# Moving the table matmuls, the gate parts and the first table's store in an attention and mixture-of-experts kernel

## The chip, the cores and the metric

The kernel runs on one core of a Trainium2 chip. The metric is the device time of one execution in microseconds. A core has TensorE (PE in the profile; PEld is its weight load), VectorE (DVE), ScalarE (ACT), GpSimd (POOL) and SyncE (SP). Each engine works through its own instructions in order. SyncE and GpSimd also issue the transfers (DMA) between DRAM and on-chip memory.

## What is computed

The reference is attention followed by a mixture of experts with one expert per token. Cut to what matters:

```
# attention: 8 batches, 8 heads, 576 positions, 64 wide
scores = q @ k.T / 8, masked (heads 0-3: the last 32 positions; heads 4-7: every 32nd)
x = softmax(scores) @ v                       # 4608 tokens x 512

do_compute = x @ w_skip > 0
logits     = xc @ w_gate                      # 8 experts
e_idx      = argmax(logits);  gate_w = softmax(logits)[e_idx]
for e in range(8):
    h = relu(xc[e_idx == e] @ w1[e])          # 512 -> 1024
    y[e_idx == e] = gate_w * (h @ w2[e])      # 1024 -> 512
out = x;  out[do_compute] = xc + y
```

## The kernel before

**The attention part** is a loop over 32 units: 8 batches (`b`) of 4 units (`pr`), where units 0 and 1 hold the heads with the local mask and units 2 and 3 those with the strided one. An iteration `n` mixes three units: the scores of unit n+2 (`qk`, L201, into the bank S), the transposes and exponentials of unit n (`tex`, L239 and L247), and the product with v of unit n-1 (`pv`, L273). VectorE adds the mask (L208, L210), which empties S, takes the maximum (L216), and divides the product by its sum (L281 to L288). GpSimd subtracts the maximum (L219). TensorE, VectorE and GpSimd are under a manual schedule here, so that their order is the order of the code.

**Routing** lies between these. A group of batches is routed when it is done: groups are batches 0-1, 2-3, 4, 5, 6 and 7 (`GROUPS`). `score` (L331) multiplies with the gate weights, `route1` makes logits, exponentials and the chosen expert on VectorE, `norm` (L386 to L388, GpSimd) adds up the exponentials into `gate`, and `route2` (L394 to L406) ranks the tokens of each expert by matmuls.

**The tables.** For each expert a table on chip (`tabs`) lists its tokens: row to read, row to write, gate weight. It is made by matmuls. `hot` (up to five tiles of 128 tokens) makes on VectorE two one-hots of a token's place, `eh` (L433) and `lo` (L445), from `hq` and `hc` (L428 to L431). It also takes the reciprocal of the gate sum (L435), which GpSimd splits into three bf16 parts (L437 to L440); GpSimd then multiplies `eh` with five columns (place, tile, three gate parts) into `hpm` (L442). `place` (L452) multiplies `lo` with `hpm` on TensorE and VectorE adds the result to `acc` (L456, L458). The list `ready` holds what `hot` has made at the end of an iteration; the next iteration places it. `tabled` (L463 to L468) turns `acc` into `tabs`.

**The tail.** The fullest expert among the first groups, "e", is computed first (`ffn1`, `ffn2`, L648 to L650), from a table of up to 288 tokens read before the last groups are known. When all groups are placed, its whole table is stored to DRAM (L977) and 128 rows behind its first ones are read back from there as a list "l" (`listed`, L613), since the place is known only at run time. `gather` (L620, GpSimd) fetches the tokens' rows, `xsplit` (L642) transposes them, and `tok1` and `tok2` compute the list. The other seven experts follow in the order of `TURN`, each with its table read by `rows` (L610) and its own gathers. Weights come in pieces of 512 KB through three buffers `raw` (`wdma`, L567, SyncE), which VectorE frees by `wrest` (L584). In the tail the scheduler orders SyncE and GpSimd; TensorE, ScalarE and VectorE stand as written.

Of the kernel before, what the change touches and what calls it, by code (L numbers as in the profile page):

```python
# [37 lines left out]
NP = 5  # L38
# [70 lines left out]
def attn_moe(ctx: ExitStack, tc: tile.TileContext, q, k, v, w9d, w1d, w2d, cst, out, NB=B):  # L109
# [279 lines left out]

    def route2(g, tag="T", of=None):  # L390
# [30 lines left out]
    def hot(a, z):  # L421
# [5 lines left out]
        q, c, r = sp("hq", []), sp("hc", []), sp("hr", [])  # L427
# [7 lines left out]
        V.reciprocal(gate[:, o], gate[:, o])  # L435
        w = [parts[:, o, i] for i in range(2, NP)]
        G.tensor_copy(w[0], gate[:, o])  # L437
        G.tensor_tensor(r, gate[:, o], w[0], op=ALU.subtract)
        G.tensor_copy(w[1], r)
        G.tensor_tensor(w[2], r, w[1], op=ALU.subtract)  # L440
# [395 lines left out]
    late, ranked, warm, ready = [], None, [], []  # L836
    pool_order = ExitStack()
    pool_order.enter_context(tc.manual_schedule(engines={G.engine, T.engine, V.engine}))
    for n, (b, pr) in enumerate(units):
# [30 lines left out]
        full = bool(ready) and ready[0][0] == GOFF[GROUPS.index((CB, CB + 1))]  # L870
        put = [] if full and pr == 0 else [place(*x) for x in ready]
        if put:
            ready = []
# [13 lines left out]
        if full and pr == 1:  # L887
            run(*put)
            tabled()
# [29 lines left out]
        if n == 1:  # L919
            G.tensor_copy(parts[:, :, 0:2], con["pk"].rearrange("p (t c) -> p t c", c=2))  # L920
        if warm and pr == (0 if warm[0][0] not in GOFF else 3 if warm[0][0] >= GOFF[GROUPS.index((CB, CB + 1))] else 2):
            ready.append(hot(*warm.pop(0)))
# [21 lines left out]
    psum, bufs = pctx.enter_context(tc.tile_pool(name="psumT", bufs=1, space=PSUM, reuse_waits="tile")), {"S": 2, "T": 3, "PV": 2, "R": 1}  # L944
    ga = ffn1a("e")
# [4 lines left out]
    run(islice(g, 4), *[place(*x) for x in ready], later(route1, nr), islice(g, 4), later(route2, nr))  # L950
    norm(nr)
    new = hot(*hots(nr)[0])
# [18 lines left out]
    s0n = nc.sync.value_load(isel[0:1, 2:3], min_val=0, max_val=(NE - 1) * ESTR + CE[0] * CE[1])  # L971
    for r in TURN:
        e = nc.sync.value_load(order[0:1, 0, r:r + 1], min_val=0, max_val=NE - 1)
        seq += [(r, e, j) for j in range(8)]
        if r == TURN[0]:
            wdma(*seq[2], 1)
            nc.sync.dma_start(tvw[bass.ds(e0, 1), 0:CMAX, :].rearrange("o (p h) c -> p (o h c)", h=3),  # L977
                              tabs[:, bass.ds(e0, 1)].rearrange("p o h c -> p (o h c)"))
        rows(r, e, *CAPS[r])
        if r == TURN[1]:  # L980
            listed("l", s0n)
    done = [0]
# [154 lines left out]
```

## Time and profile before

| | |
|---|---|
| timed runs | 463.47, 464.99, 459.25 us; median 463.47 |
| profiled execution | 461.03 us, of it the span 458.8 us |
| busy share of the span | PE 90%, DVE 61%, ACT 41%, POOL 30% |
| mean granted TensorE clock | 0.966 |
| attention part | 0 to about 190 us, the tail from there to the end |
| moved | 90.39 MB, 197 GB/s |

A row of the timeline gives the start (us from the span's start), the duration, the engine, the line, the operation with its output and inputs, and how many were merged; in brackets the idle time of the engine ahead of it and who ended it. A row of the waits view gives who waited for whom: total, times, longest. "SPq" is a transfer's issue on SyncE. The share of busy time hides that the first 190 us and the tail have different limits.

### The profile page before, as it was taken

What the parts mean: (1) busy time and instruction counts of PE and PEld (TensorE: products, weight loads), DVE (VectorE), ACT (ScalarE), POOL (GpSimd) and SP (SyncE); (2) the same over time, 40 slices, a digit from 0 to 9 for tenths busy, and PEclk for the clock granted to TensorE, in tenths of its full rate; (3) what the DMA queues carried; (4) which work ended last, traced back from release to release, by engine and by line L of the source; (5) the groups of instructions that cost most, each with busy time, mean ns of one, the idle gap of its engine ahead of it and who ended that gap; (6) DMA issues with size and microseconds to landing.
All of it is one profiled execution on the core that took longest, in us unless ns stands there. A gap on an engine that the chain in (4) does not pass through costs nothing.

```text
span 458.8 us, 12154 instructions
## 1 busy us (share of the span) xinstructions
PE 412.3 (90%) x4983; PEld 369.5 (81%) x4984; DVE 279.1 (61%) x584; ACT 187.0 (41%) x366; POOL 138.1 (30%) x190
## 2 busy tenths in 40 slices
PE   6989889889788777997999999999999999999990
PEld 3867767667576565787999799999999999999980
DVE  4666768766998878491477465464574655746410
ACT  1344354416254436541543243443543545444300
POOL 3333224541455455133113416023023030201110
PEclk8899999879999799999999999999999999999996
DMA  8999998978796323513547467556475565644110
GB/s 299 395 389 320 367 328 285 306 226 269 224 351 225 101 53 105 146 46 79 191 155 208 154 212 207 144 185 184 160 228 154 189 192 195 224 139 152 28 39 21
DMA packets 53032, 90.39 MB, mean 197 GB/s; under 512 B 9479, under 2 KB 29191, under 8 KB 52973
## 3 DMA queue, kind: packets, MB, share of 16 engines
q1 hardware_dynamic: 46541, 79.21, 52.3%
q0 software_dynamic: 6432, 10.37, 8.2%
q8 instruction: 40, 0.66, 0.6%
q14 instruction: 19, 0.16, 0.1%
HBM read 75.16 MB, written 14.92 MB: 196 GB/s over the span
## 4 chain that ended last, share of the span: by engine, by line
PE 67%; DVE 13%; DMA 9%; issue 3%; POOL 3%; ACT 2%; SPq 1%; POOLq 0%; DVEq 0%; ACTq 0%
PE S L648 15%; PE S L649 15%; PE S L650 15%; PE PV L273 5%; PE T L239 4%; PE S L201 3%; DMA vt<-in_vp_dram 3%; DVE x L288 2%; PE T L315 2%; PE T L331 2%; PE PV L740 2%; DVE mx L216 2%; PE T L642 1%; DMA kt<-in_kp_dram 1%; DMA xg<-out_dram,tab 1%
## 5 line engine op out<-in xcount | busy, mean ns | idle before, releaser
L648 PE MATMUL S<-xh,w1h 128*128 128x342 f32 (+6 forms) x248 | 78.4, 316 | 0.0
L649 PE MATMUL S<-xl,w1h 128*128 128x342 f32 (+6 forms) x248 | 76.4, 308 | 0.0
L650 PE MATMUL S<-xh,w1l 128*128 128x342 f32 (+6 forms) x248 | 76.4, 308 | 0.0
L728 POOL DMA_INDIRECT out_dram<-ot,tab x25 | 27.9, 1118 | 149.2 <-DVE ot L726 135.5
L648 PE MATMUL S<-hh,w2h 128*128 128x288 f32 (+5 forms) x192 | 59.3, 309 | 0.1
L649 PE MATMUL S<-hl,w2h 128*128 128x288 f32 (+5 forms) x192 | 57.9, 302 | 0.0
L650 PE MATMUL S<-hh,w2l 128*128 128x288 f32 (+5 forms) x192 | 57.8, 301 | 0.0
L660 ACT ACTIVATE hh<-S 128x342 fp32r<-128x342 f32 (+6 forms) x64 | 28.0, 437 | 65.7 <-PE S L650 59.3
L584 DVE TENSOR_TENSOR w1l<-raw,w1h 128x1024 fp32r<-128x1024 f32 x32 | 39.6, 1244 | 21.6 <-ACT w1h L578 21.6
L648 PEld LDWEIGHTS S<-xh,w1h 128*128 128x128 f32 x248 | 46.8, 189 | 0.6 <-issue 0.4
L649 PEld LDWEIGHTS S<-xl,w1h 128*128 128x128 f32 x248 | 46.9, 189 | 0.1
L650 PEld LDWEIGHTS S<-xh,w1l 128*128 128x128 f32 x248 | 46.8, 189 | 0.0
L219 POOL TENSOR_TENSOR sm<-sm,mx 128x480 f32<-128x480 f32 (+1 forms) x32 | 28.4, 907 | 57.2 <-DVE mx L216 28.1
L620 POOL DMA_INDIRECT xg<-out_dram,tab x25 | 31.2, 1248 | 46.5 <-DMA tab<-table 12.6
L584 DVE TENSOR_TENSOR w2l<-raw,w2h 128x1024 fp32r<-128x1024 f32 x32 | 39.0, 1224 | 9.8 <-ACT w2h L578 9.6
L661 DVE SCALAR_TENSOR_TENSOR hl<-S,hh 128x342 fp32r<-128x342 f32 (+6 forms) x64 | 30.9, 484 | 19.9 <-ACT hh L660 19.7
L201 PE MATMUL S<-kt,qt 64*64 64x54 f32 (+1 forms) x1280 | 34.3, 248 | 9.6 <-DMA kt<-in_kp_dram 3.6
L201 PEld LDWEIGHTS S<-kt,qt 64*64 64x64 f32 x1280 | 28.2, 145 | 16.8 <-DVE sm L208 4.2
L648 PEld LDWEIGHTS S<-hh,w2h 128*128 128x128 f32 x192 | 36.2, 188 | 0.4 <-DVE hl L661 0.4
L645 DVE TENSOR_TENSOR xl<-T,xh 128x288 fp32r<-128x288 f32 (+7 forms) x30 | 13.1, 468 | 38.3 <-ACT xh L644 38.3
L649 PEld LDWEIGHTS S<-hl,w2h 128*128 128x128 f32 x192 | 36.2, 189 | 0.0
L650 PEld LDWEIGHTS S<-hh,w2l 128*128 128x128 f32 x192 | 36.2, 189 | 0.0
(178 smaller groups left out, 807.5 us busy)
## 6 DMA issues: line engine op xcount, KB each, us to landing
raw<-in_w_dram SPq DMA_DIRECT2D x64, 512.0 KB
vt<-in_vp_dram SPq DMA_DIRECT2D x40, 390.0 KB
qt<-in_qp_dram SPq DMA_DIRECT2D x16, 304.0 KB
kt<-in_kp_dram SPq DMA_DIRECT2D x16, 297.0 KB
out_dram<-x SPq DMA_DIRECT2D x16, 288.0 KB
kt<-in_kp_dram SPq DMA_DIRECT2D x14, 304.0 KB
qt<-in_qp_dram SPq DMA_DIRECT2D x14, 288.0 KB
out_dram<-x SPq DMA_DIRECT2D x32, 99.0 KB
```

The source lines that it names most:

```text
L201: T.matmul(s[HP * (i ^ j):HP * (i ^ j) + HP, j, (blk - b0) * win:(blk - b0 + 1) * win], lhsT=qt[p, j, blk * nq:blk * nq + HP], rhs=kt[p, j ...
L219: G.tensor_tensor(e[:, j], sw[:, j], mx[:, j].unsqueeze(2).broadcast_to([128, b1 - b0, win]), op=ALU.subtract)
L239: T.transpose(t[:w, x * 128:(x + 1) * 128], a, ident)
L273: T.matmul(p[HP * i:HP * i + HP, bank, slot * 65:slot * 65 + 65], lhsT=pt[a:z, m, j, i ^ j, :], rhs=vt[a:z, (b0 if kind == 0 else b0 // 2) ...
L584: V.tensor_tensor(lo, raw_.pop((key, j)), hi.bitcast(F32), op=ALU.subtract)
L620: i = G.indirect_dma_start(out=xg[:s["P"], t, :], out_offset=None, in_=out[0:last, :], in_offset=bass.IndirectOffsetOnAxis(ap=s["tab"][:s[ ...
L648: T.matmul(p, lhsT=a[0], rhs=b[0], start=start, stop=False)
L649: T.matmul(p, lhsT=a[0], rhs=b[1], start=False, stop=False)
L650: T.matmul(p, lhsT=a[1], rhs=b[0], start=False, stop=stop)
L660: A.activation(s["hh"][:, f, :C], p[:, :C], AF.Relu)
L661: V.scalar_tensor_tensor(s["hl"][:, f, :C], p[:, :C], 0.0, s["hh"][:, f, :C].bitcast(F32), op0=ALU.max, op1=ALU.subtract)
L728: i = G.indirect_dma_start(out=out, in_=ot[:P], in_offset=None, bounds_check=NTOK - 1, oob_is_err=False, out_offset=bass.IndirectOffsetOnA ...
```

## The change

It has four parts.

1. A `place` now waits one iteration longer behind its `hot`, that is two in all, except for group 2 (batch 4), which stays at one.
2. The reciprocal and the three gate parts leave `hot` and become `gates`, done for a whole group at once: for batches up to 5 an iteration after the group's `norm`, for later ones right behind `norm`.
3. The store of the first expert's table and the read of the list "l" are issued by GpSimd instead of SyncE.
4. SyncE reads the seven expert numbers first, and then all tables but the first.

```diff
+    def gates(g):
+        o, nt = slice(GOFF[g], GOFF[g + 1]), tiles(g)
+        zs = gate[:, o]
+        w, r = [parts[:, o, i] for i in range(2, NP)], ap.tile([128, GT], F32, name="rr", tag="rr", bufs=1)[:, 0:nt]
+        V.reciprocal(zs, zs)
+        G.tensor_copy(w[0], zs)
+        G.tensor_tensor(r, zs, w[0], op=ALU.subtract)
+        G.tensor_copy(w[1], r)
+        G.tensor_tensor(w[2], r, w[1], op=ALU.subtract)
...
     def hot(a, z):
...
-        V.reciprocal(gate[:, o], gate[:, o])
-        w = [parts[:, o, i] for i in range(2, NP)]
-        G.tensor_copy(w[0], gate[:, o])
-        G.tensor_tensor(r, gate[:, o], w[0], op=ALU.subtract)
-        G.tensor_copy(w[1], r)
-        G.tensor_tensor(w[2], r, w[1], op=ALU.subtract)
...
-        full = bool(ready) and ready[0][0] == GOFF[GROUPS.index((CB, CB + 1))]
-        put = [] if full and pr == 0 else [place(*x) for x in ready]
-        if put:
-            ready = []
+        put = [x for x in ready if n - x[0] > (x[1] != GOFF[GROUPS.index((CB - 1, CB))])]
+        ready = [x for x in ready if x not in put]
+        full = bool(put) and put[0][1] == GOFF[GROUPS.index((CB, CB + 1))]
+        put = [place(*x[1:]) for x in put]
...
-        if full and pr == 1:
+        if full:
             run(*put)
             tabled()
...
+        if summed_up:
+            gates(summed_up.pop())
+        if g and pr == 3:
+            if b > CB:
+                gates(g[0])
+            else:
+                summed_up.append(g[0])
...
-            ready.append(hot(*warm.pop(0)))
+            ready.append((n, *hot(*warm.pop(0))))
...
+    s0n = G.value_load(isel[0:1, 2:3], min_val=0, max_val=(NE - 1) * ESTR + CE[0] * CE[1])
...
-    run(islice(g, 4), *[place(*x) for x in ready], later(route1, nr), islice(g, 4), later(route2, nr))
+    run(islice(g, 4), *[place(*x[1:]) for x in ready], later(route1, nr))
     norm(nr)
+    gates(nr)
+    run(islice(g, 4), later(route2, nr))
...
-    s0n = nc.sync.value_load(isel[0:1, 2:3], min_val=0, max_val=(NE - 1) * ESTR + CE[0] * CE[1])
+    G.dma_start(tvw[bass.ds(s0, 1), 0:CMAX, :].rearrange("o (p h) c -> p (o h c)", h=3),
+                tabs[:, bass.ds(s0, 1)].rearrange("p o h c -> p (o h c)"))
+    listed("l", s0n, eng=G)
+    eids = {}
     for r in TURN:
-        e = nc.sync.value_load(order[0:1, 0, r:r + 1], min_val=0, max_val=NE - 1)
+        eids[r] = e = nc.sync.value_load(order[0:1, 0, r:r + 1], min_val=0, max_val=NE - 1)
         seq += [(r, e, j) for j in range(8)]
         if r == TURN[0]:
+            rows(r, e, *CAPS[r])
             wdma(*seq[2], 1)
-            nc.sync.dma_start(tvw[bass.ds(e0, 1), 0:CMAX, :].rearrange("o (p h) c -> p (o h c)", h=3),
-                              tabs[:, bass.ds(e0, 1)].rearrange("p o h c -> p (o h c)"))
-        rows(r, e, *CAPS[r])
-        if r == TURN[1]:
-            listed("l", s0n)
+    for r in TURN[1:]:
+        rows(r, eids[r], *CAPS[r])
```

Where the instructions stand is set by these lists, so three places are shown in the engines' order. In the changed kernel the line numbers are a little higher: L452 is L456, L442 is L446, L435 is L394, L388 stays.

TensorE, in batch 3, where the first table matmuls stand; before:

```order
L273 MATMUL PV<-vt_981,pts 64x65 x24
L315 MATMUL T<-cs,x_1327 128x128 x4
L452 LDWEIGHTS hlo
L452 MATMUL T<-hpm,hlo 128x120
...
L201 MATMUL S<-kt_1290,qt_1287 64x54 x24
L239 MATMUL T<-cs,sm_85 96x128 x10
L273 MATMUL PV<-vt_981,pts 64x65 x20
L315 MATMUL T<-cs,x_1512 128x128 x6
L201 MATMUL S<-kt_1290,qt_1287 64x54 x20
```

And in the change:

```order
L273 MATMUL PV<-vt_981,pts 64x65 x24
L315 MATMUL T<-cs,x_1333 128x128 x4
L201 MATMUL S<-kt_1296,qt_1293 64x54 x24
L239 MATMUL T<-cs,sm_85 96x128 x10
L273 MATMUL PV<-vt_981,pts 64x65 x20
L315 MATMUL T<-cs,x_1512 128x128 x6
L456 LDWEIGHTS hlo
L456 MATMUL T<-hpm,hlo 128x120
...
L201 MATMUL S<-kt_1296,qt_1293 64x54 x20
```

The five matmuls stand an iteration later, behind the next scores, transposes and product. The same holds for the three other `hot`s of the first two groups; the matmuls of the later groups keep their places.

VectorE, in batch 6 (unit 3), where the group of batch 5 is ranked; before:

```order
L406 TENSOR_REDUCE rank<-rdd 128x5
L428 TENSOR_SCALAR hq<-rank 128x5
L429 TENSOR_SCALAR hq<-hq 128x5
L430 TENSOR_TENSOR hc<-hq,pickw 128x5
L431 SCALAR_TENSOR_TENSOR hc<-hc,rank 128x5
L433 TENSOR_TENSOR heh<-cs,hc 128x120
L435 RECIPROCAL gate<-gate 128x5
L445 TENSOR_TENSOR hlo<-cs,hq 128x640
L210 TENSOR_TENSOR sms<-S,cs 128x648
```

And in the change:

```order
L416 TENSOR_REDUCE rank<-rdd 128x5
L394 RECIPROCAL gate<-gate 128x5
L438 TENSOR_SCALAR hq<-rank 128x5
L439 TENSOR_SCALAR hq<-hq 128x5
L440 TENSOR_TENSOR hc<-hq,pickw 128x5
L441 SCALAR_TENSOR_TENSOR hc<-hc,rank 128x5
L443 TENSOR_TENSOR heh<-cs,hc 128x120
L449 TENSOR_TENSOR hlo<-cs,hq 128x640
L210 TENSOR_TENSOR sms<-S,cs 128x648
```

The reciprocal has moved from behind the one-hot `heh` to the front of the five instructions that make it.

GpSimd, at the end of the routing; before, the last product `hpm` is followed by the gathers:

```order
L442 TENSOR_TENSOR hpm<-heh,parts 128x600
L620 DMA xg<-out_dram,tab 128x512
L620 DMA xg<-out_dram,tab 114x512 x3
L728 DMA out_dram<-ot,tab 4608x512
L620 DMA xg<-out_dram,tab 114x512 x3
```

And in the change:

```order
L446 TENSOR_TENSOR hpm<-heh,parts 128x600
L985 ISA
L985 DMA table<-tabs 128x12
L617 ISA
L617 DMA tab<-table 128x4
L624 DMA xg<-out_dram,tab 128x512
L624 DMA xg<-out_dram,tab 114x512 x3
```

The store and the read of the list stand between the product and the gathers; SyncE has lost both.

More of the change, by code (lines that the diff above doesn't have):

```diff
@@ L425, in sp @@
             return ap.tile([128, RT1] + shape, dt, name=n, tag=n, bufs=1)[:, 0:nt]
-        q, c, r = sp("hq", []), sp("hc", []), sp("hr", [])
+        q, c = sp("hq", []), sp("hc", [])
         V.tensor_scalar(q, rank_[:, o], -1.0, 1.0 / 3.0, op0=ALU.add, op1=ALU.mult)
@@ L835, in attn_moe @@
     tvw = table.rearrange("(e r) c -> e r c", e=NE)
-    late, ranked, warm, ready = [], None, [], []
+    late, ranked, warm, ready, summed_up = [], None, [], [], []
     pool_order = ExitStack()
```

## The prediction

> **What bounds the kernel now.** I read the busy time by stretches first, one stretch for each batch of the attention part, cut where TensorE starts the score matmuls (L331). The columns are the stretch, its length, busy microseconds (and instructions) of PE, PEld, DVE, ACT and POOL, the granted clock, the DMA share and GB/s.
>
> ```profile
> 39.63:58.31 18.68, 16.86 (x388) 13.32 (x385) 11.92 (x26) 8.17 (x18) 6.20 (x8) 1.00 0.97 336
> 77.86:102.80 24.94, 20.72 (x401) 16.93 (x398) 17.68 (x42) 8.28 (x18) 11.02 (x19) 0.81 0.84 275
> 102.80:123.75 20.95, 18.36 (x410) 14.35 (x410) 16.15 (x46) 9.19 (x22) 6.88 (x12) 0.98 0.75 229
> 123.75:145.46 21.71, 17.90 (x413) 14.25 (x410) 20.52 (x54) 10.09 (x23) 12.79 (x23) 1.00 0.91 321
> 145.46:170.32 24.86, 18.85 (x369) 15.01 (x366) 20.08 (x55) 10.99 (x24) 11.35 (x21) 0.86 0.32 90
> 220.00:300.00 80.00, 79.51 (x493) 73.86 (x492) 43.94 (x68) 33.99 (x57) 20.80 (x16) 1.00 0.62 183
> ```
>
> A batch without table work takes 18.68 us. I call the next four (78 to 170 us) A, B, C and D; the table work of the first two groups lies in A and C. In A nothing is full: TensorE is busy for 20.72 of 24.94 us, and at a clock of 0.81. In C VectorE is busy for 20.52 of 21.71 us, so there it is the bound. Who waits, by the waits view (total, times, longest):
>
> ```profile
> PE T L452 <- POOL hpm L442: 7.2, 4, 2.3
> PE T L452 <- DVE pickw L372: 2.2, 1, 2.2
> PE T L642 <- DMA xg<-out_dram,tab: 2.8, 2, 2.6
> ```
>
> TensorE stands 9.4 us before the table matmuls (L452) and 2.8 us before the transposes of gathered rows (L642), 2.6 of it in one piece at 214.71 us. These are what the change aims at. Past that last wait TensorE is the bound: 79.51 of 80 us in the last row of the stretches.
>
> **Part 1, batch A.** The timeline of its two stalls (start, duration, engine, operation; in brackets the idle time ahead and its releaser):
>
> ```profile
> 83.47 0.95 DVE L208 TENSOR_TENSOR sm<-S,cs 128x768 f32<-128x768 f32 x1
> 85.76 0.42 PE L452 MATMUL T<-hpm,hlo 128*128 128x120 bf16 x5 [1.97 <-POOL hpm L442]
> 86.11 1.11 PE L201 MATMUL S<-kt,qt 64*64 64x54 f32 x48
> 87.15 2.37 PE L239 MATMUL T<-cs,sm 128*96 128x128 f32 x10
> 95.37 0.71 DVE L210 TENSOR_TENSOR sms<-S,cs 128x540 f32<-128x540 f32 x1
> 97.46 0.56 PE L452 MATMUL T<-hpm,hlo 128*128 128x120 bf16 x4 [2.25 <-POOL hpm L442]
> 97.95 1.88 PE L201 MATMUL S<-kt,qt 64*64 64x96 f32 x40
> 132.86 1.30 PE L239 MATMUL T<-cs,sm 128*96 128x128 f32 x10
> 142.79 1.05 PE L201 MATMUL S<-kt,qt 64*64 64x96 f32 x40
> ```
>
> With the matmuls an iteration later, TensorE goes from L315 straight to the next L201. That needs the S bank, which VectorE empties by 84.42 (83.47 + 0.95) and by 96.08 (95.37 + 0.71). L201 so starts 1.7 us earlier instead of at 86.11, and 1.9 us earlier instead of at 97.95: 3.6 us in all. Then the clock: the same ten transposes take 2.37 us behind the first stall and 1.30 in C, the same forty matmuls 1.88 behind the second and 1.05 in C.
>
> ```profile
> 82.00:86.00 4.00, 2.03 (x60) 1.61 (x58) 3.86 (x10) 1.44 (x3) 2.83 (x6) 1.00 1.02 365
> 86.00:90.00 4.00, 4.00 (x82) 3.36 (x81) 1.74 (x3) 1.46 (x3) 1.61 (x2) 0.59 1.08 391
> 98.00:102.00 4.00, 4.00 (x64) 3.45 (x65) 1.44 (x2) 0.00 (x0) 1.24 (x2) 0.50 0.79 254
> ```
>
> Half-busy stretches are followed by 0.59 and 0.50. With idle pieces of about 0.6 and 0.9 us in place of 2.0 and 2.2 I expect the clock to stay up. That gives 1.07 + 0.83 on these two rows, and at a clock of 0.50 half of the other 2.1 us up to 102 us, 1.1: 3.0 in all. The moved copy of the sum costs back 0.3, since it now stands ahead of the next one-hots on VectorE. Raw sum 6.3. It can't all be had: VectorE's 17.68 us stay, and C shows that a batch takes at least 1.2 us more than VectorE's busy time (21.71 - 20.52). So A goes from 24.94 to about 19.0: **-5.9 us**, with bounds -6.3 and -3.3 (the stalls without the clock).
>
> [...]
>
> **Part 2, batches B, C, D.** In B the reciprocal of the gates (0.2 us, as the row of L435 below) stands alone on VectorE's chain, with no work to hide it: **+0.2**. In C:
>
> ```profile
> 140.40 0.71 DVE L210 TENSOR_TENSOR sms<-S,cs 128x540 f32<-128x540 f32 x1
> 142.49 0.37 PE L452 MATMUL T<-hpm,hlo 128*128 128x120 bf16 x4 [1.97 <-POOL hpm L442]
> 149.79 1.39 DVE L584 TENSOR_TENSOR w1l<-raw,w1h 128x1024 fp32r<-128x1024 f32 x1 [1.77 <-ACT w1h L578]
> 151.63 2.82 SPq L296 DMA_DIRECT2D out_dram<-x  x2
> 157.23 1.02 DVE L288 TENSOR_TENSOR x<-PV,rc 128x384 f32<-128x384 f32 x2
> ```
>
> L201 can start at 141.11 instead of 142.79, so TensorE runs 1.7 us ahead. VectorE is full here, and gets only what it waited for: 1.77 us for ScalarE's cast, which stands behind TensorE's score matmuls. SyncE issues the store (L296) once that VectorE instruction has freed a weight buffer, and the product at 157.23 waits for the store. I take **-1.2** (bounds 0 and -1.7), carried along that chain into D. The table matmul of group 2 (the wait of 2.2 us) stays in its iteration; its product hpm starts sooner, and it lies beside the same store, so it adds nothing.
>
> In D the reciprocal moves ahead of the one-hots:
>
> ```profile
> 151.10 0.16 DVE L428 TENSOR_SCALAR hq<-rank 128x5 f32<-128x5 f32 x1
> 151.97 0.28 DVE L433 TENSOR_TENSOR heh<-cs,hc 128x120 bf16<-128x120 f32 x1
> 161.76 0.24 POOL L388 TENSOR_SCALAR gate<-gate 128x5 f32<-128x5 f32 x1
> 162.03 0.19 DVE L435 RECIPROCAL gate<-gate 128x5 f32<-128x5 f32 x1 [0.41 <-POOL gate L388]
> ```
>
> Now VectorE does the five one-hot instructions while GpSimd makes the gate sum, and waits only 0.41 us. In the change it meets the reciprocal first, waits until 162.0, and does the five after it. Queued behind it are hq to heh (151.10 to 152.25, 1.15 us), hlo and the mask of the next scores, for which TensorE waits. I price it at 1.15 less 0.05: **+1.1** (bounds +0.3, if GpSimd comes sooner, and +1.3).
>
> **Part 3, the tail.** First VectorE's chain to the table, then the transfers:
>
> ```profile
> 195.18 0.23 POOL L388 TENSOR_SCALAR gate<-gate 128x5 f32<-128x5 f32 x1
> 199.91 1.17 DVE L482 SCALAR_TENSOR_TENSOR key<-cnt,cs 1x8 f32<-1x8 f32 x1
> 201.11 0.15 DVE L519 SCALAR_TENSOR_TENSOR key<-first,key 1x8 f32<-1x8 f32 x1
> 204.43 0.20 DVE L468 TENSOR_TENSOR tabs<-tat,acc 128x24 f32<-128x24 f32 x1
> 172.28 0.78 POOL L610 DMA_DIRECT2D tab<-tabs  x1 [1.13 <-DVE tabs L468]
> 213.67 1.13 POOL L620 DMA_INDIRECT xg<-out_dram,tab  x1 [12.61 <-DMA tab<-table]
> 217.32 0.44 PE L642 MATMUL T<-cs,xg 128*128 128x128 f32 x2 [2.61 <-DMA xg<-out_dram,tab]
> ```
>
> ```profile
> 206.77 4.51 DMA table<-tabs
> 211.30 1.59 DMA tab<-table
> ```
>
> The key instruction of eight elements (L482) takes 1.17 us while GpSimd makes the product hpm, and the like one behind it (L519) 0.15. In the change the four GpSimd instructions ahead of hpm are done before, so hpm no longer meets it: 1.0 won. The reciprocal now stands ahead of the last ranks and waits for the gate sum, done at 195.41, where VectorE went on at about 195.2: with its own time some 0.4 lost. So tabs is done at 204.0 instead of 204.63. SyncE issued its store at 206.77, behind a weight load; GpSimd has nothing in front of it and I let it start at 204.35 (0.35 later). The store takes 4.5 as now, the load back 2.0 (1.59, and 0.4 since GpSimd's issue took 0.78 in the row of L610), with 0.3 and 0.8 between: the first gather starts at 212.0 instead of 213.67. The gathers of the second expert follow it at a fixed distance and release TensorE last, so all of it counts: **-1.7**. SyncE's seven register loads and table reads are as many as before; they lie beside TensorE's matmuls, and the weight load behind them now goes out sooner.
>
> ```profile
> DMA to landing us min/median/max: 2.7/4.7/8.2
> ```
>
> This row of the tables' transfers bounds a small one from both sides. With 2.7 and 2.0 the gain is 3.5; with 4.7 for both it is a loss of 1.2.
>
> [...]
>
> **Sum:** -5.9 + 0.2 - 1.2 + 1.1 - 1.7 = -7.5 us. The profiled execution took 461.03 us (span 458.8 and 2.2 around it), which gives 453.5. The three other runs are 459.25, 463.47 and 464.99; the mean of the four is 462.2, and I forecast from that: **454.7 us**.
>
> **The rivals.**
>
> The clock does not come back (chance 0.12): each low stretch has some other cause than the stall ahead of it. For it: the stall of 1.97 us in C is followed by matmuls at full speed (1.05 us). Then A gives 3.3 instead of 5.9: 457.3 us. [...]
>
> All of it comes through (0.2). For it: the idle time in A, 4.2 us of TensorE and 7.3 of VectorE, leaves room once the clock is up. A gives its raw 6.3, C 1.6, D loses 0.5, the tail gives 3.5, B loses 0.2: -10.7, 451.5 us.
>
> GpSimd's transfers are slower (0.11 at the median of 4.7 us each): the tail loses 1.2 instead of winning 1.7, 457.6 us. At the longest, 8.2 each, the first gather starts at 221.9 us, 8.2 later than now; the sum is +2.4 and the time 464.6, **slower than before** (0.05). It decides once store and load together exceed some 14 us, 6.5 now reckoned, that is 7 each. Against it: GpSimd's one plain transfer here (L610) needed 2.7.
>
> The change doing nothing of what it says can be ruled out but for a rest: four table matmul groups do stand an iteration later.
>
> **How the numbers follow.** The forecast keeps 0.52, with its own range of 452 to 457.5. To hold 8 in 10 the range takes in most of the larger gain and the two milder losses: 450 to 460. Faster by over 2% means under 453.0 of 462.2, which is about what a measurement of this kernel can tell from no change: nearly all of the larger gain and a fifth of the forecast's case, 0.30. Slower by over 2% would need more than 471, beyond even the last rival, and I leave it 0.02; within 2% is the rest, 0.68.
>
> **What would show it.** Right: no wait of the table matmuls over 0.5 us in A and C; the clock at 1.00 throughout A, and A near 19 us; a new wait of VectorE's reciprocal for the gate sum of over 1 us in D; the first gather about 1.7 us nearer to the table's last instruction than now. Wrong: a wait of equal size at L201 in the places of L452, clocks near 0.5 in A, or a gap of more than 9.3 us (213.67 - 204.43) between table and first gather.

## The result, and the profile after

The changed kernel takes 456.69 us in the median of 20 runs (452.46 to 459.55), the kernel before 462.25 us in 20 runs beside them (458.6 to 467.08). The ratio is 0.9871, with a 95% interval of 0.9844 to 0.9897: about 6.0 us less, within 2%. The forecast was 7.5 us less, 454.7 us. A ratio leaves out executions more than 1.5% above the fastest of their kernel, a median keeps them, so the two can differ. Both profiled executions of the changed kernel (this one and that of e1 below) were the longest of their series (459.55 and 457.53 us, 2.9 us above the medians of their series), so what a profile shows of it adds up to less gain than the timed runs.

The busy time by stretches, cut at the same places as before (A to D, then E, the batch behind D, and the row of the tail):

```profile
78.54:96.79 18.25, 16.92 (x396) 13.67 (x394) 17.10 (x39) 8.17 (x18) 9.24 (x11) 1.00 0.91 303
96.79:117.53 20.74, 18.09 (x416) 14.63 (x414) 16.47 (x48) 9.28 (x22) 7.88 (x17) 1.00 0.88 290
117.53:137.81 20.28, 17.53 (x409) 13.98 (x407) 19.16 (x52) 9.97 (x23) 10.98 (x18) 1.00 0.96 338
137.81:165.08 27.27, 21.10 (x372) 16.88 (x370) 20.27 (x55) 11.10 (x24) 11.57 (x19) 0.81 0.30 84
165.08:185.24 20.16, 16.76 (x191) 13.61 (x187) 13.48 (x50) 9.56 (x23) 7.93 (x15) 0.83 0.34 88
220.00:300.00 80.00, 79.71 (x479) 74.24 (x480) 44.71 (x69) 34.33 (x57) 21.86 (x16) 0.98 0.54 170
```

A went from 24.94 to 18.25 us and C from 21.71 to 20.28, with the clock at 1.00. D grew from 24.86 to 27.27 and E from 17.88 to 20.16, with the clock at 0.81 and 0.83 (0.86 and 1.00 before). The waits of TensorE:

```profile
PE S L201 <- DVE sms L210: 6.1, 4, 2.2
...
PE S L646 <- DMA xg<-out_dram,tab: 2.2, 1, 2.2
...
PE T L456 <- DVE rd L364: 1.5, 1, 1.5
...
PE T L646 <- DMA xg<-out_dram,tab: 1.1, 1, 1.1
```

The row of L201, which waits for the mask L210, was half as large before:

```profile
PE S L201 <- DVE sms L210: 3.0, 3, 1.5
```

The 7.2 us for the product hpm at the table matmuls (L452, now L456) are gone. What is left at L456 is mainly group 2's, which the change leaves in its iteration (it ended at hpm; the view names the VectorE instruction that ended then); another 0.7 us, in C, has no releaser. The wait for gathered rows (L642, now L646) has not gone: it was 2.6 us at the list's rows and 0.5 at the second expert's, and is now 1.1 and 2.2. The next rows are the timeline of TensorE: two of A, where L201 now stands in the place of the stalls, one of C, and three of D.

```profile
85.09 1.02 PE L201 MATMUL S<-kt,qt 64*64 64x54 f32 x48 [0.62 <-DVE sm L208]
...
93.80 1.15 PE L201 MATMUL S<-kt,qt 64*64 64x96 f32 x40
...
134.82 1.15 PE L201 MATMUL S<-kt,qt 64*64 64x96 f32 x40 [1.59 <-DVE sms L210]
...
157.03 1.33 PE L201 MATMUL S<-kt,qt 64*64 64x54 f32 x40 [2.25 <-DVE sms L210]
158.29 1.94 PE L239 MATMUL T<-cs,sm 128*96 128x128 f32 x8
160.16 2.44 PE L273 MATMUL PV<-vt,ptl 96*64 96x65 f32 x40
```

In C the second stall has only moved: 1.59 us at L201, for the mask, where 1.97 stood at the table matmuls. In D a new stall of 2.25 us stands at L201, and the 40 matmuls of L273 behind it take 2.44 us at a clock of 0.50 (158 to 162 us), where 40 of these take 1.39 in the kernel before at 138.44 us, at 1.00. VectorE and GpSimd in D:

```profile
154.03 0.24 POOL L388 TENSOR_SCALAR gate<-gate 128x5 f32<-128x5 f32 x1
```

```profile
154.30 0.19 DVE L394 RECIPROCAL gate<-gate 128x5 f32<-128x5 f32 x1 [2.27 <-POOL gate L388]
...
156.15 0.82 DVE L210 TENSOR_TENSOR sms<-S,cs 128x648 f32<-128x648 f32 x1
```

The reciprocal waits 2.27 us for the gate sum, and the mask (L210) for which L201 waits is queued behind it. The tail, first GpSimd and SyncE, then the chain of waits, then stretches:

```profile
201.88 0.68 POOL L985 DMA_DIRECT2D table<-tabs  x1 [5.56 <-DVE tabs L472]
204.19 0.57 POOL L617 DMA_DIRECT2D tab<-table  x1 [1.64 <-DMA table<-tabs]
209.12 1.10 POOL L624 DMA_INDIRECT xg<-out_dram,tab  x1 [4.36 <-DMA tab<-table]
...
213.53 1.18 POOL L624 DMA_INDIRECT xg<-out_dram,tab  x1 [0.30 <-issue]
```

```profile
214.19 1.89 SPq L571 DMA_DIRECT2D raw<-in_w_dram  x2
```

```profile
213.53 6.71 DMA xg<-out_dram,tab
```

```profile
213.50:220.30 6.80, 4.62 (x39) 4.41 (x37) 0.85 (x4) 1.44 (x5) 1.18 (x1) 1.00 0.87 238
220.20:224.20 4.00, 3.91 (x23) 3.91 (x24) 2.80 (x5) 2.56 (x5) 0.00 (x0) 0.63 0.08 33
```

The table's last instruction now starts at 201.38, so the first gather starts 7.74 us behind it instead of 9.24. But the last gather of the second expert takes 6.71 us from issue to landing, beside weight loads that SyncE issues from 214.19, and TensorE's clock is 0.63 behind the wait. In the kernel before the same gather took 4.95 us, and the weight loads went out at 221.87:

```profile
218.13 4.95 DMA xg<-out_dram,tab
```

### The profile page after: what moved, and what is told of

It reads as the page before. It is cut to its first block, busy times and chain, and to the rows that moved or that the text cites. A ratio compares the mean times of both kernels' runs of the same rounds, so it can differ in the third digit from the quotient of the medians.

```text
span 457.9 us, 12138 instructions
## 1 busy us (share of the span) xinstructions
PE 414.4 (90%) x4983; PEld 372.2 (81%) x4984; DVE 277.0 (60%) x582; ACT 187.1 (41%) x366; POOL 137.2 (30%) x184
## 4 chain that ended last, share of the span: by engine, by line
PE 50%; DMA 1%; POOL 0%; DVE 0%; POOLq 0%; issue 0%
PE S L652 15%; PE S L653 15%; PE S L654 15%; PE PV L744 2%; DMA xg<-out_dram,tab 1%; PE T L646 1%; PE PV L786 0%; PE PV L785 0%; PE PV L784 0%; PE S L759 0%; PE S L760 0%; PE S L761 0%; PE T L771 0%; POOL out_dram L732 0%; PE S L646 0%; PE PV L646 0%
## 5 line engine op out<-in xcount | busy, mean ns | idle before, releaser
L201 PE MATMUL S<-kt,qt 64*64 64x54 f32 (+1 forms) x1280 | 34.1, 247 | 13.3 <-DVE sms L210 6.1
L201 PEld LDWEIGHTS S<-kt,qt 64*64 64x64 f32 x1280 | 28.3, 145 | 20.3 <-DVE sms L210 7.7
```

The costliest lines, as they stand in the source:

```text
L201: T.matmul(s[HP * (i ^ j):HP * (i ^ j) + HP, j, (blk - b0) * win:(blk - b0 + 1) * win], lhsT=qt[p, j, blk * nq:blk * nq + HP], rhs=kt[p, j ...
```

## The experiments

All are compared with runs of the kernel before on the same chip. Line numbers shift by a few with an edit. The table has the stages of every profile, worked out from the starts of the score matmuls (L331), and, in the last two columns, the landing time of the gather that TensorE waited for last (the second expert's last one; in e2, e6 and e8, where no wait for its rows shows, the list's) and the time from the end of the table's last instruction to the end of the span (before: 458.8 - 204.63 = 254.17).

| kernel | ratio (95% interval) | A | B | C | D | E | gather | table to end |
|---|---|---|---|---|---|---|---|---|
| before | | 24.94 | 20.95 | 21.71 | 24.86 | 17.88 | 4.95 | 254.17 |
| the change | 0.9871 (0.9844 to 0.9897) | 18.25 | 20.74 | 20.28 | 27.27 | 20.16 | 6.71 | 256.32 |
| e1 the change again | 0.9847 (0.9787 to 0.9906) | 18.25 | 20.73 | 21.61 | 25.54 | 17.58 | 6.78 | 256.28 |
| e2 tail by SyncE | 0.9881 (0.9821 to 0.9940) | 18.25 | 20.74 | 20.29 | 26.38 | 19.25 | 3.63 (list) | 254.88 |
| e3 tail alone | 0.9976 (0.9933 to 1.0019) | 22.59 | 20.47 | 23.08 | 24.87 | 17.92 | 7.58 | 257.10 |
| e6 later places alone | 0.9859 (0.9811 to 0.9908) | 18.39 | 20.69 | 21.69 | 24.71 | 17.69 | 3.65 (list) | 254.31 |
| e4 late gates behind | 0.9841 (0.9796 to 0.9886) | 18.25 | 20.73 | 20.28 | 24.90 | 20.16 | 7.14 | 256.59 |
| e5 places as before | 0.9892 (0.9855 to 0.9930) | 18.68 | 20.53 | 21.06 | 26.47 | 20.92 | 7.33 | 255.36 |
| e7 weights held | 0.9818 (0.9776 to 0.9861) | 18.25 | 20.74 | 20.30 | 26.36 | 22.23 | 5.10 | 252.58 |
| e8 stalls filled | 0.9997 (0.9967 to 1.0028) | 21.54 | 20.49 | 23.73 | 24.77 | 20.51 | 3.47 (list) | 254.89 |
| e9 both mends | 0.9823 (0.9779 to 0.9867) | 18.25 | 20.73 | 20.29 | 24.91 | 20.11 | 4.64 | 252.82 |
| e10 tail alone, weights held | 0.9956 (0.9921 to 0.9992) | 21.04 | 20.49 | 23.23 | 24.78 | 20.70 | 4.91 | 253.09 |
| e11 both mends, D filled | 0.9800 (0.9761 to 0.9840) | 18.25 | 20.74 | 21.48 | 24.20 | 20.42 | 5.01 | 252.93 |
| e12 both mends, store held | 0.9816 (0.9774 to 0.9858) | 18.24 | 20.74 | 20.27 | 24.89 | 17.71 | 4.99 | 253.04 |

**e1, the change once more.** No edit.

> The whole change once more, for a second profile. In the first one A took 18.25 us (24.94 before), but D 27.27 (24.86), E, the batch behind D, 20.16 (17.95), and the part behind it 272.66 (270.60), with the granted clock low in pieces of D, E and the tail. Theory: D's cost belongs to the change (the reciprocal waits 2.3 us for the gate sum and a low clock follows), so D is 26 us or more again; E's and the tail's losses are a clock that fell by chance, so E is under 18.5 and the tail under 271.5. Rival: all three belong to the change, E stays at 20 and the tail above 272. Time by both about 456.

454.68 us against 460.01. D is 25.54, longer than before again, if short of the 26 of both theories. E is 17.58, so its loss in the first profile is no fixed cost. The part behind it is 272.61 (256.28 from the table), as in the first profile (272.66), so that loss belongs to the change: there the rival held.

**e2, the tail's transfers by SyncE as before.**

```diff
-    G.dma_start(tvw[bass.ds(s0, 1), 0:CMAX, :]...
-    listed("l", s0n, eng=G)
+    nc.sync.dma_start(tvw[bass.ds(e0, 1), 0:CMAX, :]...
...
+        if r == TURN[1]:
+            listed("l", s0n)
```

> Later table matmuls and earlier gate parts, but the table's store and the list's load go through SyncE as before. Theory of the prediction: the two transfers through GpSimd bring the first gather nearer by 1.0 to 1.5 us, all on the path: this kernel is 1.0 to 1.5 us slower than the whole change. Rival: the gathers then run beside the second expert's weight loads, which SyncE now issues at 214 instead of 222 us, and land later by as much: this kernel takes the same time as the whole change, within 0.5 us.

454.09 us, where e1 took 454.68 in the same series; by the ratios (0.9881 against 0.9871 and 0.9847) it is 0.5 to 1.6 us slower than the change. The intervals overlap, so the timed runs do not tell theory from rival. The profile speaks for the rival: the first gather comes 1.5 us later behind the table's last instruction (9.2 us against 7.7), but TensorE no longer waits for the second expert's rows, whose last gather took 6.7 to 6.8 us; its last wait is for the list's gather, which lands in 3.63, and the table is 254.88 us from the end, 1.4 nearer than in the change.

**e3, the tail's part alone**, on the kernel before.

```diff
-            nc.sync.dma_start(tvw[bass.ds(e0, 1), 0:CMAX, :]...
+    G.dma_start(tvw[bass.ds(s0, 1), 0:CMAX, :]...
+    listed("l", s0n, eng=G)
...
-        if r == TURN[1]:
-            listed("l", s0n)
```

> The kernel before with only the tail's part: store of the first expert's table and load of the list by GpSimd, SyncE's loads in the new order. Theory of the prediction: 0.7 us for the table's earlier VectorE chain is not in it, the rest is: 1.0 to 1.5 us faster than before, 461. Rival (contention with the weight loads): no change, within 0.5 us of before.

460.96 us against 460.01, ratio 0.9976 (0.9933 to 1.0019): no gain that can be measured, though the 1.0 to 1.5 us of the theory lie within the interval too. In the profile it is a loss, 257.10 us from table to end, with the gather at 7.58 us, as the rival has it.

**e6, the later places alone**, on the kernel before.

```diff
-        put = [] if full and pr == 0 else [place(*x) for x in ready]
+        put = [x for x in ready if n - x[0] > (x[1] != GOFF[GROUPS.index((CB - 1, CB))])]
+        ready = [x for x in ready if x not in put]
...
+        put = [place(*x[1:]) for x in put]
```

> The kernel before with the table matmuls an iteration later and nothing else; reciprocal and gate parts stay behind the one-hots. Theory of the prediction: the later matmuls alone take the stalls out of A (19 us) and C, and D keeps the reciprocal's wait of 0.4 us and stays below 25 us, so this is 1 us or more faster than the same with the gates ahead (the kernel with the SyncE tail). Rival: without the earlier gate parts the product comes late for the later matmul too; A keeps a wait of over 1 us and the kernel is slower than the one with the gates ahead.

454.12 us, ratio 0.9859: as fast as the whole change. A takes 18.39 us and D 24.71. The gate parts made ahead and the tail's part together bring nothing on top that the runs can show. That it beats the kernel with the gates ahead (e2) by 1 us cannot be told from the timed runs: the medians are equal (454.12 and 454.09), the ratios 0.9859 and 0.9881 with intervals that overlap. In the profiles D is 1.7 us shorter.

**e4, the late groups' gates behind the one-hots again.**

```diff
-            if b > CB:
-                gates(g[0])
-            else:
+            if b <= CB:
                 summed_up.append(g[0])
...
+        if g is not None:
+            gates(g)
         pm = sp("hpm", [NP, 24], BF16)
```

> The whole change, but for the group of batch 5 and the one behind it the reciprocal and the gate parts stand behind the one-hots again, as before. Theory: the reciprocal's wait for the gate sum is what D loses, so D goes back from 25.5 to 27.3 us (three profiles with the gates ahead) to 24.7 to 24.9 (the three with the gates behind), and the kernel is 1 to 2 us faster than the whole change. Rival: D's length is set by the stores and the clock, whatever stands ahead; D stays above 25.5 and the time as it is.

The first rows are VectorE's and TensorE's in D:

```profile
153.03 0.19 DVE L394 RECIPROCAL gate<-gate 128x5 f32<-128x5 f32 x1 [0.41 <-POOL gate L388]
```

```profile
154.72 0.80 PE L201 MATMUL S<-kt,qt 64*64 64x54 f32 x40 [0.58 <-DVE sms L210]
```

The wait is 0.41 us again, L201's 0.58, the 40 matmuls behind it are fast (0.80 us, 1.33 in the change), and D is 24.90. So the order in D is the cause: the five profiles with the gates ahead have 25.54 to 27.27 (mean 26.4), the eight with them behind and nothing filled in D 24.71 to 24.91 (mean 24.8). The time, 0.9841, is not to be told from the whole change's; this execution lost in E, as the change's first did.

**e5, the places as before, the gates ahead.**

```diff
-        put = [x for x in ready if n - x[0] > (x[1] != GOFF[GROUPS.index((CB - 1, CB))])]
-        ready = [x for x in ready if x not in put]
-        full = bool(put) and put[0][1] == GOFF[GROUPS.index((CB, CB + 1))]
+        full = bool(ready) and ready[0][1] == GOFF[GROUPS.index((CB, CB + 1))]
+        put = [] if full and pr == 0 else ready
+        if put:
+            ready = []
```

> The whole change, but the table matmuls stay in the iteration of before. Theory of the prediction: the later place is what takes the stalls away; here the matmuls still wait for the product, though GpSimd starts it some 2 us sooner, and A stays above 21 us; about 2 to 4 us slower than the whole change. Rival: GpSimd's four gate instructions ahead of the product were the whole stall of 2 us, so that it goes with the gates alone and A takes under 20 us, as fast as the whole change.

```profile
83.38 0.42 PE L456 MATMUL T<-hpm,hlo 128*128 128x120 bf16 x5 [0.80 <-POOL hpm L446]
...
92.36 0.37 PE L456 MATMUL T<-hpm,hlo 128*128 128x120 bf16 x4 [1.08 <-POOL hpm L446]
```

The two stalls of A, 1.97 and 2.25 us, shrink to 0.80 and 1.08, and A takes 18.68 us. The rival was nearly right: either part alone takes most of what A lost, and together they bring A 0.4 us more. About 0.2 of that is only moved into B, where four of A's table matmuls now stand (B is 20.53 here and 20.74 in the change). In C the later place still counts (a wait of 2.18 us is left at L456 there, C is 21.06). The time is 457.28 us, ratio 0.9892; that it is slower than the change (0.9871) the overlapping intervals do not show.

**e7, the second expert's next weight loads behind its gathers.**

```diff
-            wdma(*seq[done[0] + 2], seq[done[0] + 2][2] + 1)
+            wdma(*seq[done[0] + 2], seq[done[0] + 2][2] + 1, st_[TURN[0]]["taken"] if done[0] < 3 else ())
```

> The whole change, but the second expert's next weight loads wait until its rows have been gathered. Theory: the last gather takes 6.7 to 7.6 us with the store and list on GpSimd and 3.6 to 5.0 on SyncE because two weight loads of 512 KB run beside it; held back, it lands in 5 us or less, TensorE's wait of 2.2 us for it goes, the clock stays at 1.00 behind it, and the part from the table's last instruction to the end shrinks from 256.5 to below 255: 1.5 to 3 us faster than the whole change. Rival: the gather is slow for another reason (its own descriptors behind the list's load): landing stays above 6 us, and the time as it is or longer, with the weights late.

The chain of waits, the waits of TensorE behind the table, and two stretches:

```profile
212.63 5.10 DMA xg<-out_dram,tab
```

```profile
PE S L646 <- DMA xg<-out_dram,tab: 0.6, 1, 0.6
```

```profile
212.60:217.70 5.10, 4.58 (x38) 4.37 (x36) 0.80 (x4) 1.39 (x5) 1.18 (x1) 1.00 0.49 129
219.00:223.00 4.00, 4.00 (x34) 3.82 (x33) 2.80 (x6) 2.67 (x6) 0.00 (x0) 1.00 0.81 272
```

During the gather the DMA engines are 0.49 busy instead of 0.87; it lands in 5.10 us (4.95 in before; the 3.6 of the expectation is the list's gather), the wait of 2.2 us is down to 0.6, the clock is 1.00 behind it, and the weight loads come afterwards. From table to end it is 252.58 us, 3.7 less than in the change. 454.14 us against 462.23, 0.9818: better than the change's 0.9871, though the intervals just overlap. In the profile the theory of the crowded gather held.

**e8, the stalls of A filled**, on the kernel before: eleven matmuls on zeros ahead of each of A's two place groups; no wait is taken away.

```diff
+        for _ in range(fill):
+            T.matmul(w[:, 128:512].rearrange("p (a b) -> p a b", b=128), lhsT=dummy,
+                     rhs=dummy.unsqueeze(1).broadcast_to([128, 3, 128]), start=True, stop=True)
```

> The kernel before with eleven matmuls of 384 columns on zeros ahead of each of the two table matmul groups of A, on the same bank, so that TensorE is busy for most of the time that it waited; they do no work for the output. Theory: the clock of 0.59 and 0.50 comes from the stall ahead of it; filled, the clock stays at 1.00, A takes 22.5 to 23.5 us instead of 24.94 though nothing starts sooner, and the kernel is 1 to 2 us faster than before. Rival: the low clock has another cause; it stays near 0.5 behind the filled stalls, A is 24.5 us or longer and the time unchanged or worse.

```profile
82.59 1.95 PE L453 MATMUL T<-dummy 128*128 128x384 bf16 x11
84.73 0.42 PE L456 MATMUL T<-hpm,hlo 128*128 128x120 bf16 x5 [0.20 <-POOL hpm L442]
85.09 0.92 PE L201 MATMUL S<-kt,qt 64*64 64x54 f32 x48
85.94 1.30 PE L239 MATMUL T<-cs,sm 128*96 128x128 f32 x10
```

```profile
86.00:90.00 4.00, 3.61 (x96) 3.07 (x96) 2.64 (x8) 2.11 (x5) 1.44 (x2) 1.00 0.95 327
```

The clock stays at 1.00, the ten transposes take 1.30 us instead of 2.37, and A takes 21.54 instead of 24.94. But the time is the same, 462.16 us. The profile of e10 (below), which has the kernel before's attention part unfilled, tells why this proves less than I meant it to:

```profile
84.94 0.42 PE L452 MATMUL T<-hpm,hlo 128*128 128x120 bf16 x5 [1.98 <-POOL hpm L442]
...
95.10 0.37 PE L452 MATMUL T<-hpm,hlo 128*128 128x120 bf16 x4 [2.26 <-POOL hpm L442]
```

```profile
85.00:89.00 4.00, 4.00 (x109) 3.44 (x108) 2.52 (x9) 1.39 (x4) 1.61 (x2) 1.00 1.08 375
```

The same two stalls, and the clock is 1.00 behind both; A is 21.04. Of the same six stalls in three profiles (before, e3, e10) three are followed by a low clock: two in before (0.59 and 0.50, A 24.94), one in e3 (the ten transposes take 2.37 us there too, A 22.59), none in e10. So the stalls of 2.0 to 2.3 us did not always bring the clock down here, and filling them has no sure gain. Other stretches have other odds. At the second place of C, e10 and e8 stall for 2.25 and 2.48 us and the clock falls behind it (the five matmuls of L315 there take 1.33 us), and before and e5 stall for 1.97 and 2.18 and it does not (0.76 for the same five). Behind the wait for group 2 in D, 1.52 to 2.20 us, the 48 matmuls of L201 take 1.54 to 1.64 us in before, the change, e5 to e10 and e12, where 48 take 0.92 at a clock of 1.00 (e10, in A); it is 0.50 from 155 to 160 us in before and from 150 to 153 us in the change.

**e9, both mends**, those of e4 and e7, on the changed kernel.

```diff
+            if b <= CB:
                 summed_up.append(g[0])
...
+            wdma(*seq[done[0] + 2], seq[done[0] + 2][2] + 1, st_[TURN[0]]["taken"] if done[0] < 3 else ())
```

> The whole change with both mends: the late groups' gate parts behind their one-hots, and the second expert's next weight loads behind the gathers of its rows. Theory: the two add up, since they lie in different stretches. D is 24.9 us, the part from the table's last instruction to the end 252.6, and the kernel is 1.5 to 3 us faster than the whole change and 8 to 9 us faster than before (ratio 0.981). Rival: what is won in D is lost in E to a low clock, and the kernel is as fast as the one with the held weights alone (0.9818) or slower.

455.02 us against 461.84, 0.9823. In the profile the two do add up, D 24.91 and 252.82 us from table to end, with a span of 451.6 us. The timed gain over the weights held alone (0.9818) is nil within the interval; 0.9823 against the change's 0.9871 is 2 us.

**e10, the tail alone with the weights held**, on the kernel before: e3 and one line more.

```diff
+            wdma(*seq[done[0] + 2], seq[done[0] + 2][2] + 1, st_[TURN[0]]["taken"] if done[0] < 3 else ())
```

> The kernel before with the tail's part (store and list by GpSimd) and the next weight loads held behind the gathers; the attention part is as before. Theory: the tail's part without the contention is worth what the prediction gave it: the end is 252.5 to 253 us behind the table's last instruction, where it is 254.2 to 254.9 with the SyncE tail and 255.4 to 257.1 with the GpSimd tail; 1.5 to 2.5 us faster than before. Rival: the gain behind the table in the earlier profile with held weights was a clock by chance; 254 us or more, no change against before.

459.47 us against 461.84, ratio 0.9956 (0.9921 to 0.9992): faster, by some 2 us, with 253.09 us from table to end. With the gather free of the weight loads, the tail's part is worth about what the prediction gave it. The 4 us by which the two profiles differ from table to end (e3: 257.10) are not found in the timed runs, which differ by 0.2%, with intervals that overlap.

**e11, D filled too**: e9, with eight matmuls on zeros ahead of group 2's place and three behind it.

```diff
+        if a == GOFF[2]:
+            fill_in(w, 8)
...
+        if a == GOFF[2]:
+            fill_in(w, 3)
```

> The same with both mends, and eight matmuls of 384 columns on zeros ahead of the table matmuls of group 2 and three behind them, in D, where TensorE waits 1.5 us for the product and the clock falls to 0.50 in every profile so far; they do no work for the output. Theory: filled, the clock stays up in D, and D takes 22.5 to 23.5 us instead of 24.9, 1 to 2 us off the time of the kernel with both mends. Rival: VectorE, the gate sum and the stores set D; the clock is up but D stays above 24.4 and the time the same.

```profile
148.00:152.00 4.00, 3.17 (x98) 2.67 (x98) 3.82 (x11) 1.46 (x3) 1.31 (x2) 1.00 0.08 22
```

```profile
155.22 0.80 PE L201 MATMUL S<-kt,qt 64*64 64x54 f32 x40 [2.29 <-DVE sms L210]
```

The clock is 1.00 throughout D, where it falls in the nine profiles named under e8 (0.81 over D in the change, 0.86 in e9); that speaks for the wait for group 2 as what brings it down there. But D is 24.20, only 0.7 less: the time that TensorE wins it waits at the next L201, 2.29 us, for VectorE, which in the 4 us up to 152 is busy for 3.82 and then itself waits 0.41 us for the gate sum. The rival of a D set by VectorE and the gate sum holds for most of it. Ratio 0.9800 (0.9761 to 0.9840), 453.46 us; its interval lies below that of the change.

**e12, a store of the last batch behind the first expert's gathers**, on e9.

```diff
-    store(NB - 1, 0)
+    store(NB - 1, 0, st_["e"]["taken"])
```

> The kernel with both mends, and the last batch's store of its first half waits until the first expert's rows have been gathered. In E the two run together and the DMA engines are 0.9 busy; in nine of thirteen profiles TensorE stands there with pieces of idle time that nothing in the profile explains, the clock falls to 0.50, and E takes 19.3 to 22.2 us, in the other four 17.6 to 17.9. Theory: the pieces come from the crowd of transfers; with the store held back E takes under 18.2 us and the kernel is 1.5 to 2.5 us faster than the one with both mends (0.9823 of before). Rival: the gathers alone or something else holds TensorE up; E stays at 19 us or more, or the later store costs elsewhere, and the time is not lower.

TensorE in E, in the changed kernel's first profile and in e12:

```profile
169.85 0.92 PE L273 MATMUL PV<-vt,pts 54*64 54x65 f32 x44 [0.16 <-ACT pts L247]
171.29 0.30 PE L273 MATMUL PV<-vt,pts 54*64 54x65 f32 x3 [0.53 <-issue]
172.05 0.26 PE L273 MATMUL PV<-vt,pts 54*64 54x65 f32 x1 [0.45 <-issue]
...
176.12 1.57 PE L273 MATMUL PV<-vt,pts 54*64 54x65 f32 x40 [0.79 <-ACT xT L317]
```

```profile
166.10 0.98 PE L273 MATMUL PV<-vt,pts 54*64 54x65 f32 x48 [0.17 <-ACT pts L247]
...
170.02 0.92 PE L273 MATMUL PV<-vt,pts 54*64 54x65 f32 x40 [1.55 <-ACT xT L319]
```

In the first, 48 matmuls come in pieces with idle time that no instruction explains, and the next 40 run at about half speed (1.57 us instead of 0.92). In e12 they come in one piece, and E is 17.71. The span, 448.4 us, is the shortest of all profiles and the median, 451.00 us, the lowest; but against the kernel before in the same series (460.01) the ratio is 0.9816, as without the edit (0.9823). And one good E proves little where four of thirteen were good without it, one of them (before) with the DMA engines 0.92 busy from 176 to 180 us, as against 0.94 from 171 to 175 us in the change. The nine long ones are not all alike either: in eight TensorE stands in pieces, in e2 (19.25) it does not: there the twelve matmuls of L646 take 2.75 us (1.53 in e1), some way behind a wait of 1.55 us that the good ones have too (1.55 to 1.62). Whether the store causes the pieces stays open.

## Why the prediction was right, and where its steps were off

The time fell inside the range, and the gain, 6.0 us, is the forecast's less 1.5. That it came so near is in part luck: by the profiles the terms add up to 3.3 us only, as shown below, and the rest is not accounted for. Of its signs of being right, three came: the clock at 1.00 throughout A, the reciprocal's wait in D, and the nearer gather. The waits at the table matmuls went too, but for 0.73 us in C. Of the signs of being wrong one came for C alone, the wait at L201 in the place of L452. The terms, one by one, in us, with the table above:

**A, -5.9.** The mechanism is shown: the stalls go (0.62 and none where 1.97 and 2.25 were), the clock is 1.00 in A in the change, e9, e11 and e12, and the other five profiles with the later places are as short (18.24 to 18.39 in all nine), and A is 18.25 where "about 19.0" stood; VectorE's busy time there fell too, to 17.10, and the 1.2 above it that bounded the term holds. But the starting point was one execution. With no low clock at all (e10) A was 21.04 before, so the stalls alone are worth 2.8 (3.3 was given as the bound without the clock), and each low clock some 1.5 to 2.4 more. The mean of the three unfilled profiles is 22.86, which makes A worth 4.6, some 0.2 of it moved into B. The step that failed is taking the clock of the one profile for that of every run. The rival "the clock does not come back" fell; a milder form of it, that in many runs it never went, was not among the cases.

**B, +0.2.** 20.74 against 20.47 to 20.49 in the three other profiles with places and gates as before: +0.25. The number is right by luck, the cause is another. With the gates ahead and the places as before (e5) B is 20.53, so the reciprocal costs next to nothing; with the places alone (e6) it is 20.69. What B pays for are the four table matmuls that the change moves into it from A, 3.2 us behind its start.

**C, -1.2.** 20.72 in the mean of the nine profiles with the later places, against 22.94 in the four with places and gates as before (21.71 to 23.73): -2.2, more than the bound of -1.7. But the clock is in it: it is down in e10 (0.93), e8 (the 40 score matmuls behind the stall take 1.68 us instead of 1.05), e11 (0.92) and e6 (the 40 take 1.97), and by their lengths in e3 and e1: in three of these four and in three of the nine. Of like clock, C is worth 1.4 where it is 1.00 (21.71 against 20.27 to 20.30) and some 1.8 where it is down, so the term was sized right. The profile of before had C's best case, as it had A's worst. VectorE sets the pace as reckoned: TensorE comes sooner and waits 1.59 us for its mask.

**D, +1.1.** The wait came, and larger, 2.27 us instead of 0.41; the mean cost is 1.6. The prediction counted the one-hots that queue behind the reciprocal, not the clock, which is 0.50 from 157 to 163 us, behind TensorE's stall of 2.25 us. Its price for the queue was right: the mask L210 starts 1.85 us behind the reciprocal's start (154.30 to 156.15) instead of 0.81 (162.03 to 162.84), 1.04 later. The rows at 151.10 and 151.97 that it shows for the one-hots are those of the group ahead; its own run from 159.67 to 161.62 beside the gate sum, in 1.95 us, and that is why the wait grew to 2.27. e4 shows the cause of the loss, the order; how much of it is the clock is not told apart.

**Tail, -1.7.** Here the forecast failed, though its own sign came true: the first gather does come 1.5 us nearer. In parts: VectorE's chain was to be 0.6 sooner; from the score matmuls to the table it is 16.34 us where it was 16.43, 0.1 sooner. The key instruction (now L486) does take 0.16 instead of 1.17, but the slowing has only moved: hpm now runs beside VectorE's w2l, which takes 1.85 us where it took 1.23. With the reciprocal's wait, w2l starts 10.31 us behind the score matmuls instead of 10.02. So 1.0 is won and 0.9 lost. Before, and in the change:

```profile
198.22 1.23 DVE L584 TENSOR_TENSOR w2l<-raw,w2h 128x1024 fp32r<-128x1024 f32 x1
```

```profile
195.55 1.85 DVE L588 TENSOR_TENSOR w2l<-raw,w2h 128x1024 fp32r<-128x1024 f32 x1
```

```profile
194.70 1.62 POOL L446 TENSOR_TENSOR hpm<-heh,parts 128x600 bf16<-128x600 bf16 x1 [0.91 <-DVE heh L443]
```

The two transfers by GpSimd take 7.24 us up to the first gather (201.88 to 209.12) where SyncE's took 6.90 (206.77 to 213.67), 0.34 more; 7.65 was reckoned. They win by not queueing behind SyncE's weight load: the store is issued 0.30 us behind the table's last instruction, where SyncE's was 2.14 behind, after a weight load at 206.14. The rival "GpSimd's transfers are slower" fell. Its bounds came from the wrong rows: the 4.7 and 8.2 us are of a view in which the gathers (L620, 3.2 to 8.2 us) and the row stores (L728, 2.7 to 6.7) are 50 of 51 transfers, and the one table took 2.7.

What failed is the sentence "The gathers of the second expert follow it at a fixed distance and release TensorE last, so all of it counts". They start at a fixed distance (the last one 4.46 us behind the list's in before, 4.41 in the change), but they land later: the last one in 6.7 to 7.6 us in the five profiles with the GpSimd tail, in 4.95 in before, and in 4.6 to 5.1 in the five with the weights held; in e2, e6 and e8, with SyncE's tail, no wait for them shows. The text itself named the cause ("the weight load behind them now goes out sooner") and priced it at nothing. Nor did the second expert's rows bound the wait before: of TensorE's 3.1 us there 2.6 were for the list's, and now 2.2 of 3.3 are for the second expert's. From table to end the means of the profiles are 256.3, 254.6 and 252.9 us: the tail's part cost 1.8 instead of winning 1.1, and wins 1.7 once the loads are held back. The timed runs do not confirm the loss (e3 is at 0.9976, e2's ratio is no better than the change's).

**The sum** of these means is -4.6 + 0.2 - 2.2 + 1.6 - 0.1 + 1.8 = -3.3 us, where the timed runs say -6.0. The change's two profiled executions lay 2.9 us above the medians of their series, so its stages may look worse than in most runs; where in a faster run time is saved no profile shows. Two places to look are the tail, whose loss the timed runs do not show, and E, 17.6 to 22.2 us with no order that follows the edits. That stays open.

So the gain is the attention part's. Of the four parts of the change one, the later places, makes all of it that the runs can show (e6); the gates ahead would have done nearly as much for A (e5) and cost 1.6 us in D; the tail's part brings no gain that could be measured until the weight loads are held back. The fourth part, SyncE's order, was never tried apart from the third. The version with both mends and e12's store had the lowest times; e11 is the one whose interval is clear of the change's.

## What to carry to other kernels

A transfer that is brought forward must be priced at its landing, among whatever else then runs (here 6.71 us instead of 4.95): list what its old queue will issue in the freed place, and ask which of the two is needed first. Two remedies for one stall need not add up (A was 18.39 us with the later places alone, 18.68 with the gates ahead alone, 18.25 with both); try each alone, since the one that is left over may only cost (here the reciprocal ahead of a wait). And a clock that is low in one profile is one draw (here behind three of six like stalls in A): price the stall and the clock apart, and give the stall alone as the sure part.

## What the runs showed of the hardware

- In A, stalls of 2.0 to 2.3 us on TensorE were followed by a low granted clock in three of six cases of the same code: 0.59 and 0.50 in before, and in e3, by the same ten transposes, which took 2.37 us instead of 1.30. In e10 it was 1.00 behind both. With the two stalls filled by matmuls on zeros (e8) it was 1.00 behind the first, and behind the second 40 matmuls took 1.06 us instead of 1.88. In D, behind waits of 1.52 to 2.20 us for group 2, 48 matmuls took 1.54 to 1.64 us in nine profiles (before, the change, e5 to e10, e12), 0.92 in e10's A at a clock of 1.00; the clock was 1.00 where the wait was filled (e11).
- A gather of 114 rows by GpSimd landed in 4.95 us where the weight loads of 512 KB from SyncE's queue came in its last 1.2 us (before), in 4.6 to 5.1 where they were held back, and in 6.7 to 7.6 beside them.
- The same small table went to memory in 2.3 us by GpSimd (201.88 to 204.19) and 4.5 by SyncE, and the list came back, up to the first gather, in 4.9 us by GpSimd (204.19 to 209.12) and 2.4 by SyncE (211.30 to 213.67). GpSimd for the one and SyncE for the other was not tried.
- In E TensorE stood in pieces, idle for 0.2 to 0.6 us at a time with nothing to wait for, in eight of thirteen profiles; in the change the DMA engines were 0.94 busy from 171 to 175 us, and the clock was 0.50 from 174 to 180 us. In the other five it did not stand in pieces, in before with the DMA engines 0.92 busy from 176 to 180 us and the clock at 1.00.
- VectorE's w2l of 128x1024 took 1.23 us, and 1.85 beside GpSimd's hpm; the key instruction of 1x8 took 0.16, and 1.17 beside it.
